# Down products of an MLP: seven products on quarters for eight pairs of feature chunks, and a gate by one SiLU

## Chip, cores and metric

One core of a Trainium2 chip. The time is the device time of one execution in microseconds, the median of several runs; the shares come from one profiled execution. TensorE (PE) multiplies, VectorE (DVE) and ScalarE (ACT) do elementwise work, GpSimd (POOL) a few small steps and the accumulating transfers, SyncE (SP) issues most of the other DMAs.

## The reference, cut to what matters

x is 2048 rows by 512 columns, all in float32; F is 1376.

```python
xn = layernorm(x)
s = linear_attention(xn, wqkv, wo)         # 32 heads of 16, features max(t,0)+exp(min(t,0))
hs = shift(gelu(layernorm(xn) @ w1)) @ w2  # quarters of the columns shifted by +1, -1, +2, -2 rows
x1 = xn + hs
h2 = gelu(layernorm(x1) @ w3) @ w4         # the MLP: 512 -> 1376 -> 512
out = x + s * silu(x1 + h2)
```

## The kernel before, in words

The kernel writes down some 5000 operations in a program order and lets a planner of its own (`Plan`, lines 88 to 395) choose the issue order. Every operation has an engine, a busy time and a latency by formula. TensorE's operations get a nominal time by adding their busy times up; the others get a due time from the operation that needs them. `emit` then goes forward, and takes again and again the operation that can start first, by due time among those. A DMA has a modelled landing. A TensorE operation that opens a new PSUM bank may go ahead of its place by 6 us at most, and only while two banks are free. `SOONER` moves single due times by hand. What comes out is a fixed instruction stream for each engine, with semaphores between.

Buffers come from pools: "p" has 96 of 128 x 516 words, for nearly everything; "h" six of 256 columns; PSUM has four banks "acc" and four "mm". A load into a "p" buffer is issued at most about 14 us ahead of need, and later when few buffers are free.

Precision: every float32 matrix is split into a rounded high part and the rest, and a product is three matmuls, high by high, high by low, low by high (`products`, line 478). All matmuls stand on line 148, so the profile tells them apart by tiles: the left name of a row is the PSUM tile.

Rows are worked in four blocks of 512 rows, a block being four tiles of 128. Up to about 228 us the kernel does the attention's sums over all rows (k, q, the Gram matrix g) and the token mixing (h, and the w2 product); x1 is kept in DRAM (`x1d`), its layer norm, turned, too. Then the loop at line 1441 does the MLP of the four blocks, one after the other. F is eleven chunks of 128 features, the last of 96; five pairs (s, s + 5) and the last alone. For each block:

- `up_last` (line 1133): the last chunk's up product, PSUM tile `a`, 24 matmuls of 256 columns.
- `up_pair` (line 1149): the up product of one pair of chunks by Strassen's scheme in Winograd's form (`seven`, line 883): seven products of 256 x 256 blocks for eight, each two contraction chunks by three split matmuls, 42 matmuls of 256 columns, in three banks (`pa`, `pb`, `pe`). Results go through GELU on ScalarE twice, once to the high part and once in full, and the low part is their difference.
- `down` (line 1168): the down product of a chunk, 512 columns wide, for the four row tiles, summed over all eleven chunks in four banks `acc`. The chunks of a group are issued one group after their up product; the last two groups (three in block 3) at the end.
- `turn_q`, `forms_q`, `attend_pair`: the attention's output for two row tiles each, again by `seven` (tiles `pas`, `pbs`, `pes`, result `so`), among groups two to five.
- `gate` (line 1246): x1 is fetched (`xo`) and added to the bank, then th = tanh(t/2), so = so * t, th = (th + 1) * so. The factor 1/2 of the SiLU stands in the mask of the attention (line 1403). x is added by an accumulating DMA on POOL's queue or, for the last two tiles, by VectorE, and the tile is stored.

In block 3 the fourth tile is summed in two halves of 256 columns, the second in a bank `accx` of its own, with x1 added there by an identity matmul: the last gate works on a half tile straight from PSUM.

w3's forms stay in buffers through all blocks; w4's split parts are made in block 0, kept in DRAM (`w4d`) and fetched again for each block (`load_w4`, line 1107), four transfers of 256 KB per pair.

Of the kernel before, what the change touches and what calls it, by code (L numbers as in the profile page):

```python
# [82 lines left out]
class Op:  # L83
    __slots__ = ("eng", "busy", "lat", "emit", "pre", "post", "tiles", "opens", "two", "table", "patience", "soon", "loads",
                 "nom", "due", "ready", "at", "end", "mb", "order")


class Plan:
# [9 lines left out]
    def add(self, eng, busy, lat, reads, writes, emit, two=False, table=None, mb=0.0):  # L98
# [4 lines left out]
        op.patience, op.soon = self.patience, False  # L103
# [55 lines left out]
    def act(self, out, src, func, scale=1.0, bias=None, total=None):  # L159
        nc = self.nc  # L160
        psum = out.tile.psum or src.tile.psum
        lat = (.15 if psum else .195) + out.n / 1200
        lat += .092 * (isinstance(scale, View) + isinstance(bias, View)) + (.095 if total is not None else 0)
        table = 0 if func == AF.Exp else 1 if func in (AF.Gelu_apprx_tanh, AF.Tanh) else None

        def emit():
            kw = {} if bias is None else {"bias": get(bias)}
            if total is not None:
                kw["accum_out"] = total.get()
            nc.scalar.activation(out.get(), src.get(), func, scale=get(scale), **kw)  # L170

        self.add("ACT", lat - .1, lat, [src, scale, bias], [out] + ([] if total is None else [total]), emit, table=table)
# [32 lines left out]
    def load(self, out, src, eng="SP"):  # L205
        mb = out.n * P * 4 / 1e6
        e = self.nc.scalar if eng == "ACT" else self.nc.sync
        self.add(eng, .42, 0, [], [out], lambda: e.dma_start(out.get(), src), mb=mb)

    def store(self, dst, src):  # L210
        mb = src.n * P * 4 / 1e6
        if isinstance(dst, View):
            return self.add("SP", .42, 0, [src], [dst], lambda: self.nc.sync.dma_start(dst.get(), src.get()), mb=mb)
        else:
            self.add("SP", .42, 0, [src], [], lambda: self.nc.sync.dma_start(dst, src.get()), mb=mb)

    def fetch(self, out, src):

        mb = out.n * P * 4 / 1e6
        self.add("SP", .42, 0, [src], [out], lambda: self.nc.sync.dma_start(out.get(), src.get()), mb=mb)  # L220

    def gather(self, out, src, share=1.0):

        mb = out.n * P * 4 / 1e6 * share
        return self.add("POOL", .8, 0, [src, out], [out],
                 lambda: self.nc.gpsimd.dma_start(out.get(), get(src), accum_op=ALU.add), mb=mb)  # L226

# [42 lines left out]
    def emit(self, first, lead, reserve, window, ahead, table=()):  # L270
# [20 lines left out]
        while left:  # L291
# [70 lines left out]
            if op.mb:  # L362
                soft = e == "POOL"
                late = min(.92, 1.03 * max(0.0, dma - s))
                dma = max(dma, s + (.97 if soft else .06)) + op.mb * (4.59 if soft else 3.43)
                op.end = max(dma + (1.89 if soft else 1.29) + late, s + (4.08 if soft else 2.08 if op.loads else 2.2))
                under[soft].pop(0)
                under[soft].append(op.end)
# [30 lines left out]
def linear_attn_gated_by_mixer(  # L399
# [29 lines left out]
    EARLY = (), ()  # L429
    SUMS = "DVE"  # L430
# [8 lines left out]
    counts = {"w": 2, "p": 96, "h": 6, "sm": 10, "ab": 2, "acc": 4, "mm": 4}  # L439
# [202 lines left out]
    def join_a(b):  # L642

        t = ABC[b] = pl.new("ab", f"abc{b}", F32, BT + W)
        a = EDGE + b * BT - 2
        pl.fetch(t.all, arow[:, a:a + BT + W].via(lambda ap: ap.to_broadcast([P, BT + W])))
# [32 lines left out]
    def make_u(b):  # L679

        m = piece(f"um{b}")
        pl.fetch(m, mrow[:, b * BT:(b + 1) * BT].via(lambda ap: ap.to_broadcast([P, BT])))
# [58 lines left out]
    class Turned:  # L741
# [15 lines left out]
        def take(self):  # L757
# [3 lines left out]
            for n in range(nb):  # L761
# [4 lines left out]
                pl.fetch(dst, src)  # L766
# [212 lines left out]
    x1d = {i: memory(f"x1d{i}") for i in range(NT)}  # L979
# [18 lines left out]
    def mixed(i, xv):  # L998
# [4 lines left out]
        pl.store(x1d[i].all, xv)  # L1003
# [26 lines left out]
    w3d = {s: memory(f"w3d{s}", NF * 512) for s in range(NS)}  # L1030
    w4d = {f: memory(f"w4d{f}", 1024) for f in range(FB)}
    AF3, W4, YT, H3 = {}, {}, {}, {}
# [74 lines left out]
    def load_w4(b, f):  # L1107
        n = rows(f)
        if b == 0 and f not in early_f:
# [3 lines left out]
        for k, v in enumerate(W4[b, f]):  # L1113
            pl.fetch(v.f32, w4d[f][:n, k * 512:(k + 1) * 512])

# [33 lines left out]
    def up_pair(b, s):  # L1149
        hi, lo = zip(*(rounds(f"f{b}_{f}") for f in (s, s + NS)))  # L1150
        full = [piece(f"gf{b}_{f}") for f in (s, s + NS)]
        c1, c2 = full
# [15 lines left out]
    def down(b, f, j, a, c=0, wd=512):  # L1168
        hi, lo, n = H3[b, f]
        left = both((hi.rows(n), lo.rows(n)), j * P, (j + 1) * P)  # L1170
        products(a[:, :wd], [left + both(W4[b, f], c, c + wd)], f == FIRST, f == FINAL)

# [65 lines left out]
    def attend_pair(i):  # L1238
        o1, o2 = SO[i], SO[i + 1] = piece(f"so{i}"), piece(f"so{i + 1}")
        ps = seven(f"s{i}", [o1.cols(0, TH), o1.cols(TH, 512), o2.cols(TH, 512)],  # L1240
                   lambda x, y: [QF[i][x][c] + M[y][c] for c in range(2)])
        pl.act(o2.cols(0, TH), ps, AF.Copy)

    XO, XR, GT, XL = {}, {}, {}, {}

    def gate(i, a, o=0, w=512, late=False, by_dma=True, whole=False):
        cs = o, o + w
        if o == 0:
            XO[i], GT[i] = XL.get(i) or piece(f"xo{i}"), piece(f"th{i}")
            if late and i not in XL:  # L1250
                pl.fetch(XO[i], x1d[i].all)
            if not by_dma:
                XR[i] = piece(f"xr{i}")
                pl.load(XR[i], x[i * P:(i + 1) * P, :])
        t, so, th = XO[i].cols(*cs), SO[i].cols(*cs), GT[i].cols(*cs)
        if whole:
            t = a[:, :w]
        elif late:
            pl.tt(t, a[:, :w], t, ALU.add)
        else:  # L1260
            pl.act(t, a[:, :w], AF.Copy)
            pl.gather(t, x1d[i].all, 1.4)
# [3 lines left out]
        if by_dma:  # L1266
            pl.gather(th, x[i * P:(i + 1) * P, :])
        else:
            pl.tt(th, th, XR[i].cols(*cs), ALU.add)
        pl.store(out[i * P:(i + 1) * P, o:o + w], th)  # L1270
# [99 lines left out]
    fill = [lambda f=f: make_w4(f) for f in early_f] + [lambda s=s: make_pair(s) for s in early_s]  # L1370
# [32 lines left out]
    pool(.4, [], bmask.all, lambda: g.memset(bmask.all.get(), 0.5))  # L1403
# [31 lines left out]
    while fill:  # L1435
        fill.pop(0)()
    turn_y(0)
    load_last()
    load_w4(0, FB - 1)
    load_pair(0)  # L1440
    for b in range(NQ):
        A = [pl.new("acc", f"acc{b}_{j}", F32, 512) for j in range(QT)]
        last = b == NQ - 1
        B = [(A[-1], 0), (pl.new("mm", "accx", F32, 512), D // 2)] if last else []
        groups = [(FB - 1,)] + [(s, s + NS) for s in range(NS)]
        keep = 3 if last else 2
        for n, fs in enumerate(groups):
            if b == 0 and 0 < n < NS:
                load_pair(n)
            if n < NS:  # L1450
                for f in groups[n + 1]:
                    load_w4(b, f)
            elif not last:
                load_w4(b + 1, FB - 1)
            if n == 0:
                up_last(b)
            else:
                up_pair(b, n - 1)
            if b == 0 and n == 1:
                forms_m()  # L1460
            pairs = []
            if n > 0:
                for k in range(2):
                    if n == (2, 3)[k]:
# [3 lines left out]
                    if n == (4, 5)[k]:  # L1468
                        pairs.append(b * QT + 2 * k)
            if n > 0 and n - 1 < len(groups) - keep:  # L1470
                for f in groups[n - 1]:
                    for j in range(QT - len(B) // 2):
                        down(b, f, j, A[j])
                    for a, o in B:
                        down(b, f, QT - 1, a, o, D // 2)
                    while pairs:
                        attend_pair(pairs.pop())
            while pairs:
                attend_pair(pairs.pop())
        rest = [f for fs in groups[len(groups) - keep:] for f in fs]  # L1480
        if not last:
            turn_y(b + 1)
            for f in rest:
                for j in range(QT):
                    down(b, f, j, A[j])
            for j in range(QT):
                gate(b * QT + j, A[j], late=True)
        else:
            i, (a, o) = b * QT + QT - 1, B[-1]
            XL[i] = piece(f"xo{i}")  # L1490
            pl.fetch(XL[i], x1d[i].all)
            t = piece(f"xi{i}", F32R)
            hi, lo = t.cols(0, TH), t.cols(TH, 512)
            rounded(hi, lo, XL[i].cols(o, o + TH))
            pl.patience = 0.0
            for j in range(QT - 1):
                for f in rest:
                    down(b, f, j, A[j])
                gate(b * QT + j, A[j], late=True, by_dma=j < 2)
            for a, o in B:  # L1500
                if o:
                    for v in (hi, lo):
                        pl.mm(a[:, :TH], identr.all, v, False, False)
                for f in rest:
                    down(b, f, QT - 1, a, o, D // 2)
                gate(b * QT + QT - 1, a, o, D // 2, late=True, by_dma=False, whole=o > 0)

    SOONER = (
# [3 lines left out]
    )  # L1512
    pl.emit(first=6.0, lead={"p": 14.0, "w": 14.0, "ab": 10.0}, reserve={"p": 20, "w": 1, "ab": 0}, window=12.0,
# [38 lines left out]
```

## Time and profile before

| | us |
|---|---|
| Time before, median of 3 runs | 514.07 (512.39 to 514.64) |
| The profiled execution, its time | 512.43 |
| Its span (first to last instruction) | 510.7 |
| TensorE busy | 502.9 |
| VectorE busy | 426.3 |
| ScalarE busy | 348.9 |

Busy time of TensorE counts from the start of a matmul to its modelled end; since matmuls overlap, a run of them is measured by its whole length over its count. The windows view gives each engine's busy time in a stretch, and behind it, in brackets, the number of its instructions. Rows of a timeline read: start, duration, engine and line, operation, output <- inputs, shape.

### The profile page before, as it was taken

The numbers are of one execution on the slowest core, as the hardware profiler recorded it, in microseconds if no ns is written. First come the engines' busy times: TensorE is split into PE (matmuls) and PEld (weight loads), VectorE is DVE, ScalarE is ACT, GpSimd is POOL, SyncE is SP. The second block draws the span as 40 slices with busy tenths as digits, with TensorE's granted clock in tenths as the row PEclk, the third lists the DMA queues.
The fourth block names the chain that finished last, engine by engine and source line by source line (L and its number), as shares of the span: only waits on it lengthen the run. The fifth ranks groups of instructions, "written<-read, shape, count | busy, mean of one in ns | idle before, by whom it ended". The sixth has DMA issues, their size and how long they took to land.

```text
span 510.7 us, 8948 instructions
## 1 busy us (share of the span) xinstructions
PE 502.9 (98%) x2972; PEld 437.9 (86%) x2972; DVE 426.3 (83%) x885; ACT 348.9 (68%) x703; POOL 91.2 (18%) x145
## 2 busy tenths in 40 slices
PE   9998999999999999999999999999999999999995
PEld 7777777898888788889989898999898998999985
DVE  6999999999699986999999978956779656898645
ACT  5899699676697785866876668655488453765621
POOL 1258411663134122021000020000020000200000
PEclk9999999999999999999999999999999999999999
DMA  8889947189994799799767758475495595758604
GB/s 270 310 185 226 303 151 167 41 201 295 278 284 92 239 292 270 199 271 313 247 204 205 224 137 280 160 215 154 164 230 183 181 222 166 182 185 265 195 14 111
DMA packets 76619, 106.17 MB, mean 208 GB/s; under 512 B 8224, under 2 KB 31292, under 8 KB 76572
## 3 DMA queue, kind: packets, MB, share of 16 engines
q1 hardware_dynamic: 68940, 91.70, 56.4%
q0 software_dynamic: 7632, 13.90, 16.1%
q8 instruction: 23, 0.38, 0.3%
q14 instruction: 24, 0.20, 0.1%
HBM read 67.41 MB, written 29.77 MB: 190 GB/s over the span
## 4 chain that ended last, share of the span: by engine, by line
PE 86%; DVE 5%; ACT 5%; DMA 2%; issue 1%; SPq 1%; DVEq 0%; ACTq 0%
PE acc L148 23%; PE pb L148 11%; PE h L148 8%; PE g L148 7%; PE pbk L148 6%; PE pe L148 5%; PE pbm L148 4%; PE pbs L148 4%; PE pek L148 3%; PE pa L148 3%; PE pem L148 2%; PE a L148 2%; PE pes L148 2%; DMA y_1t<-y_1d 2%; PE pak L148 1%
## 5 line engine op out<-in xcount | busy, mean ns | idle before, releaser
L226 POOL DMA_DIRECT2D th<-in_x x14 | 12.2, 939 | 248.0 <-DVE so L192 64.8
L170 ACT ACTIVATE th<-xo 128x512 f32<-128x512 f32 (+1 forms) x16 | 9.8, 620 | 26.8 <-DVE xo L192 26.6
L192 DVE TENSOR_TENSOR xo<-acc,xo 128x512 f32<-128x512 f32 (+1 forms) x16 | 10.5, 671 | 16.9 <-PE acc L148 16.8
L170 ACT ACT_TABLE_LOAD x18 | 23.1, 1283 | 1.1 <-PEq L1543 0.8
L170 ACT ACTIVATE gf<-gf 128x512 f32<-128x512 f32 (+1 forms) x40 | 20.6, 525 | 0.8
L226 POOL DMA_DIRECT2D o<-x x16 | 14.0, 873 | 40.1 <-DVE o L192 15.5
L226 POOL DMA_DIRECT2D zacc<-kr x16 | 13.9, 867 | 40.6 <-DMA zacc<-kr 22.2
L170 ACT ACTIVATE p<-pb 128x256 f32<-128x256 f32 x20 | 7.6, 382 | 14.2 <-PE pb L148 14.0
L604 POOL TENSOR_TENSOR rs<-w,nhalf 128x4 f32<-128x4 f32 (+2 forms) x10 | 10.1, 1012 | 35.5 <-DVE w L197 32.6
L170 ACT ACTIVATE p<-pe 128x256 f32<-128x256 f32 x20 | 7.7, 385 | 11.9 <-PE pe L148 11.9
L170 ACT ACTIVATE ht<-ht 128x512 f32<-128x512 f32 x16 | 9.7, 623 | 8.9 <-DVE ht L192 8.9
L192 DVE TENSOR_TENSOR gf<-pa,p 128x256 f32<-128x256 f32 x20 | 8.4, 420 | 7.8 <-PE pa L148 7.5
L170 ACT ACTIVATE x<-x,nm,rs 128x512 f32<-128x512 f32 x16 | 12.9, 807 | 2.5 <-DVE nm L202 2.5
L598 DVE BATCH_NORM_STATS2 st<-o 128x6 f32<-128x512 f32 x16 | 10.9, 686 | 3.5 <-DMA o<-x 3.4
L192 DVE TENSOR_TENSOR gf<-u,pe 128x256 f32<-128x256 f32 x20 | 8.2, 410 | 6.5 <-PE pe L148 6.5
L202 DVE SCALAR_TENSOR_TENSOR kr<-kt,kr 128x512 f32<-128x512 f32 x16 | 10.9, 688 | 1.8 <-ACT kt L170 1.7
L170 ACT ACTIVATE y<-o,nm,rs 128x512 f32<-128x512 f32 x16 | 11.9, 807 | 0.5 <-DVE nm L202 0.5
L192 DVE TENSOR_TENSOR ht<-h,abc 128x512 f32<-128x512 f32 x16 | 10.9, 683 | 0.8 <-PE h L148 0.6
L202 DVE SCALAR_TENSOR_TENSOR pq<-pq,qr 128x512 f32<-128x512 f32 x12 | 8.1, 683 | 4.1 <-ACT pq L170 4.0
L170 ACT ACTIVATE u<-pb 128x256 f32<-128x256 f32 x20 | 7.7, 383 | 5.5 <-PE pb L148 5.5
L202 DVE SCALAR_TENSOR_TENSOR th<-th,so 128x512 f32<-128x512 f32 (+1 forms) x17 | 10.9, 653 | 0.5
L202 DVE SCALAR_TENSOR_TENSOR pq<-pq,rd 128x512 f32<-128x512 f32 x16 | 10.9, 688 | 0.2
(1679 smaller groups left out, 2235.5 us busy)
## 6 DMA issues: line engine op xcount, KB each, us to landing
w_s<-in_w SPq DMA_DIRECT2D x28, 256.0 KB, 4.3
x<-in_x SPq DMA_DIRECT2D x16, 256.0 KB, 5.3
zacc<-kr POOLq DMA_DIRECT2D x16, 256.0 KB, 5.9
o<-x POOLq DMA_DIRECT2D x16, 256.0 KB, 4.9
x1d<-o SPq DMA_DIRECT2D x16, 256.0 KB, 4.2
xo<-x1d SPq DMA_DIRECT2D x16, 256.0 KB, 5.0
xt<-in_xt SPq DMA_DIRECT2D x15, 256.0 KB, 5.0
out<-th SPq DMA_DIRECT2D x15, 256.0 KB, 3.4
```

Of the source, the lines that this page charges most:

```text
L148: lambda: nc.tensor.matmul(out.get(), lhs.get(), rhs.get(), start=start, stop=stop, skip_group_check=more))
L170: nc.scalar.activation(out.get(), src.get(), func, scale=get(scale), **kw)
L192: self.vec(eng, out, [a, b], lambda: self.e(eng).tensor_tensor(out.get(), a.get(), b.get(), op=op), True)
L202: lambda: self.nc.vector.scalar_tensor_tensor(out.get(), a.get(), get(s), b.get(), op0=op0, op1=op1),
L226: lambda: self.nc.gpsimd.dma_start(out.get(), get(src), accum_op=ALU.add), mb=mb)
L598: pl.add("DVE", .62, .69, [xv], [st], lambda: nc.vector.bn_stats(st.get(), xv.get()))
L604: lambda: g.tensor_tensor(out.get(), src.get(), nh.get(), op=ALU.pow))
```

## The change

In blocks 1 to 3 the down product of a pair is done by the same seven-product scheme, over row halves, the two chunks, and column halves: two pairs in block 1, three in block 2, three in block 3 (`SEVENS`), ahead of the last chunk and the ordinary pairs. Each product is two row tiles by three split matmuls of 256 columns. Four of the seven are summed over the pairs, straight in four accumulators that each hold a quarter of the block (256 rows x 256 columns in the two halves of one bank); a11 b11 is summed in a fifth bank from "mm". At the last pair of a block a chain follows in that bank: its content is copied out for quarter 11, s2 t2 of all pairs is added, it is copied for 12, s3 t3 is added, and it is copied for 21 and 22. x1 is added to these copies by accumulating DMAs. The remaining chunks of blocks 1 to 3 are added to the quarter accumulators with 256-column matmuls (`plain`).

The left forms are sums of GELUs, so a pair now makes a11, a12, a22 and s1 to s4, each split; the right forms t1 to t4 of w4 are made once (`make_t4`), t1 and t4 used at once, all four kept in DRAM (`w4t`).

The gate takes one SiLU on ScalarE and one multiply on VectorE; the mask holds 1.0. In blocks 1 to 3 it works on quarters.

The planner gets other DMA rates by kind of transfer, SiLU as a third table, 98 buffers in "p" (two that held `abc` apart join it), and another `SOONER` list.

```diff
-    counts = {"w": 2, "p": 96, "h": 6, "sm": 10, "ab": 2, "acc": 4, "mm": 4}
+    counts = {"w": 2, "p": 98, "h": 6, "sm": 10, "acc": 4, "mm": 4}
+    SEVENS = 0, 2, 3, 3
+    FIRST7 = 1
-        table = 0 if func == AF.Exp else 1 if func in (AF.Gelu_apprx_tanh, AF.Tanh) else None
+        table = {AF.Exp: 0, AF.Gelu_apprx_tanh: 1, AF.Silu: 2}.get(func)
+    RATE = {"load": 2.92, "fetch": 3.5, "row": 4.18, "turn": 5.7, "store": 2.44, "gather": 5.79}
+    def make_t4(b, s):
+        r1, r2 = piece(f"w4_{s}_s0"), piece(f"w4_{s}_s1")
+        for r, f in ((r1, s), (r2, s + NS)):
+            pl.load(r, w4[f * P:(f + 1) * P, :])
...
+        right([r.cols(k * TH, (k + 1) * TH) for r in (r1, r2) for k in range(2)], lambda k: place[k])
+        for n, (src, a, z) in enumerate(((fa, "t1", "t4"), (fb, "t2", "t3"))):
+            hl = rounds(f"w4_{s}_{n}")
+            rounded(*hl, src)
...
+    def load_group(b, s):
...
+        for name in ("b11", "t4", "b21", "t1", "b22"):
+            load_form(b, s, name)
+    def up_pair(b, s):
+        if s >= SEVENS[b]:
+            up_plain(b, s)
+            return
...
+        ps = seven(f"{b}_{s}", z, lambda x, y: [AF3[s][x][c] + YT[b][y][c] for c in range(2)])
...
+        def keep(name, v, src):
+            t = piece(f"f{b}_{s}{name}", F32R)
+            f[name] = t.cols(0, TH), t.cols(TH, 512)
+            pl.act(f[name][0], src, AF.Gelu_apprx_tanh)
+            pl.act(v, src, AF.Gelu_apprx_tanh)
+            split(f[name][1], v, f[name][0])
+        pl.act(z[1], z[1], AF.Gelu_apprx_tanh)
+        keep("a11", z[0], z[0])
+        pl.tt(n3, z[0], z[1], ALU.subtract)
+        keep("a22", z[2], z[2])
+        pl.tt(n1, z[1], z[2], ALU.add)
+        pl.tt(n2, n1, z[0], ALU.subtract)
+        hl = rounds(f"f{b}_{s}t")
+        rounded(*hl, s23)
...
+        keep("a12", z[3], ps)
+        pl.tt(n4, z[3], n2, ALU.subtract)
+        hl = rounds(f"f{b}_{s}s")
+        rounded(*hl, s14)
...
+    STREAM = ("a1", "a11", "b11"), ("a4", "a22", "t4"), ("a2", "a12", "b21"), ("a5", "s1", "t1"), ("a3", "s4", "b22")
+    CHAIN = None, ("s2", "t2"), ("s3", "t3")
+    def into(regs, left, right, first):
+        for j in range(2):
+            out, own = regs[j]
+            start = first and (own or j == 0)
+            products(out, [both(left, j * P, (j + 1) * P) + right], start, more=not start,
+                     behind=out.tile.all if first else None)
+    def stream(b, acc, s, which=STREAM):
+        for a, x, y in which:
+            into(acc[a], F4[b, s][x], G4[b, s, y], s == 0)
+    def plain(b, acc, f, which):
+        hi, lo, n = H3[b, f]
+        for a in which:
+            t, d = QUARTER[a]
+            left = both((hi.rows(n), lo.rows(n)), t * TH, (t + 1) * TH)
+            into(acc[a], left, both(W4[b, f], d * TH, (d + 1) * TH), False)
+    def downs(b, acc, s, which=("a4", "a2", "a5", "a3")):
...
+            if s < SEVENS[b] - 1:
+                stream(b, acc, s)
+            else:
+                for n in range(3):
+                    stream(b, acc, s, (STREAM[:1], STREAM[1:3], STREAM[3:])[n])
+                    chain(b, n)
+                c = piece(f"c5_{b}")
+                pl.act(c, acc["a5"][0][0].tile.all, AF.Copy)
+                pl.tt(EV[b]["12"], c, EV[b]["12"], ALU.add)
...
+    def chain(b, n):
...
+        for s in range(SEVENS[b]) if n else ():
+            x, y = CHAIN[n]
+            load_form(b, s, y)
+            into(UC[b], F4[b, s][x], G4[b, s, y], False)
+        for k in (("11",), ("12",), ("21", "22"))[n]:
...
+            pl.act(e[k], t.all, AF.Copy)
+            pl.gather(in2(e[k]), x1)
-        pl.act(th, t, AF.Tanh, scale=0.5)
-        pl.tt(so, so, t, ALU.mult)
-        pl.stt(th, th, 1.0, so, ALU.add, ALU.mult)
+        pl.act(th, t, AF.Silu)
+        pl.tt(th, th, so, ALU.mult)
-    pool(.4, [], bmask.all, lambda: g.memset(bmask.all.get(), 0.5))
+    pool(.4, [], bmask.all, lambda: g.memset(bmask.all.get(), 1.0))
-        groups = [(FB - 1,)] + [(s, s + NS) for s in range(NS)]
+        n7 = SEVENS[b]
+        groups = list(range(n7)) + ["last"] + list(range(n7, NS))
```

In block 3 each quarter is finished by itself and gated while the next is summed (`a2`, `a5`, `a3`, then the two row halves of `a4`, the second in a bank of its own with x1 from an identity matmul).

More of the change, by code (lines that the diff above doesn't have):

```diff
@@ L977, in mixer @@
         forms(b)
-    x1d = {i: memory(f"x1d{i}") for i in range(NT)}
+    x1d = [memory(f"x1d{b}", 512, QT * P) for b in range(NQ)]
     YD = {}
@@ L1002, in mixed @@
         moments(f"st2{i}", xv, mv2[:, 2 * i:2 * i + 2])
-        pl.store(x1d[i].all, xv)
+        pl.store(x1d[b].cut([(j * 512, (j + 1) * 512)], 512, lambda ap: ap[j * P:(j + 1) * P, :]), xv)
         if j < QT - 1:
@@ L1238, in attend_pair @@
     def attend_pair(i):
[L1239 to L1255, printed above, removed]
+        b, k = divmod(i, QT)
@@ L1274, in linear_attn_gated_by_mixer @@
+        pl.act(th, t, AF.Silu)
+        pl.tt(th, th, so, ALU.mult)
+        j0, j1 = o // TH, (o + w) // TH
+        if xr is None:
+            pl.gather(in2(th), quarter(x, b, h, d, j0, j1))
+        else:
+            pl.tt(th, th, xr.cols(o, o + w), ALU.add)
+        pl.store(quarter(out, b, h, d, j0, j1), in2(th))
     warm = bank("warm")
@@ L1478, in linear_attn_gated_by_mixer, with whole @@
[L1478 to L1481, printed above, removed]
+                downs(b, acc, groups[n - 1])
+            for k in range(2):
+                if n == SAT[b][k]:
+                    attend_pair(b * QT + 2 * k)
+        rest = groups[len(groups) - keep:]
+        def whole(k):
+            return acc[k][0][0].tile.all
+        if b < FIRST7:
             turn_y(b + 1)
-            for f in rest:
-                for j in range(QT):
-                    down(b, f, j, A[j])
+            for s in rest:
+                downs(b, acc, s)
@@ L1486, in linear_attn_gated_by_mixer @@
             for j in range(QT):
-                gate(b * QT + j, A[j], late=True)
-        else:
[L1489 to L1492, printed above, removed]
+                gate_tile(b, j, acc[j].all)
+        elif not last:
+            turn_y(b + 1)
+            for s in rest:
+                downs(b, acc, s)
+            gate(b, 0, 0, whole("a2"))
+            gate(b, 1, 1, whole("a5"))
+            gate(b, 0, 1, whole("a3"))
+            gate(b, 1, 0, whole("a4"))
+        else:
+            e = EV[b]
+            xr = {}
+            for h, d in ((0, 1), (1, 0)):
+                xr[h, d] = piece(f"xr{h}{d}")
+                pl.load(in2(xr[h, d]), quarter(x, b, h, d))
+            t = piece("xi", F32R)
@@ L1493, in linear_attn_gated_by_mixer @@
             hi, lo = t.cols(0, TH), t.cols(TH, 512)
-            rounded(hi, lo, XL[i].cols(o, o + TH))
+            rounded(hi, lo, e["21"].cols(TH, 512))
             pl.patience = 0.0
[L1496 to L1501, printed above, removed]
-                    for v in (hi, lo):
[L1503 to L1506, printed above, removed]
+            for a, h, d in (("a2", 0, 0), ("a5", 1, 1), ("a3", 0, 1)):
+                for s in rest:
+                    downs(b, acc, s, (a,))
+                gate(b, h, d, whole(a), xr=xr.get((h, d)))
@@ new lines, in linear_attn_gated_by_mixer @@
+            for j in range(2):
+                r = acc["a4"][j][0]
+                if j:
+                    for v in (hi, lo):
+                        pl.mm(r, identr.all, v, False, False, more=True)
+                for s in rest:
+                    for f in (FB - 1,) if s == "last" else (s, s + NS):
+                        ah, al, n = H3[b, f]
+                        left = both((ah.rows(n), al.rows(n)), TH + j * P, TH + (j + 1) * P)
+                        products(r, [left + both(W4[b, f], 0, TH)], False, more=True)
+                gate(b, 1, 0, r, j * TH, TH, xr=xr[1, 0], whole=j > 0)
```

211 lines of the change are left out of this document (147 added, 64 removed), and 7 rows, old and new, of the table SOONER.

## The prediction

> **What bounds the kernel now.** First the page: the span, the busy time of each engine, and the chain that ended last.
>
> ```profile
> span 510.7 us, 8948 instructions
> PE 502.9 (98%) x2972; PEld 437.9 (86%) x2972; DVE 426.3 (83%) x885; ACT 348.9 (68%) x703; POOL 91.2 (18%) x145
> ...
> PEclk9999999999999999999999999999999999999999
> ...
> PE 86%; DVE 5%; ACT 5%; DMA 2%; issue 1%; SPq 1%; DVEq 0%; ACTq 0%
> ```
>
> TensorE is busy for 502.9 of 510.7 us at the full granted clock, and the chain lies on it. The waits of TensorE and the windows of the four MLP blocks (228 to 297, 297 to 366, 366 to 436, 436 to 505.6 us) say where the other 7.8 us are. The window's columns are PE, PEld, DVE, ACT and POOL busy, then clock, DMA share and GB/s.
>
> ```profile
> PE h L148 <- ACT w_0h L170: 1.3, 1, 1.3
> PE warm L148 <- POOL ones L511: 1.0, 1, 1.0
> PE pbs L148 <- ACT u2s L170: 0.3, 1, 0.3
> ```
>
> ```profile
> 228.00:297.00 69.00, 69.00 (x452) 62.25 (x450) 65.69 (x135) 47.57 (x107) 2.23 (x2) 1.00 0.76 237
> 297.00:366.00 69.00, 69.00 (x452) 62.40 (x451) 50.52 (x101) 43.30 (x90) 3.50 (x4) 1.00 0.65 189
> 366.00:436.00 70.00, 69.69 (x453) 62.42 (x452) 51.31 (x102) 43.14 (x90) 3.50 (x4) 1.00 0.70 187
> 436.00:505.60 69.60, 69.60 (x486) 64.31 (x484) 50.11 (x101) 37.52 (x83) 5.22 (x6) 1.00 0.58 165
> 505.60:510.70 5.10, 0.00 (x1) 0.00 (x0) 1.30 (x4) 0.38 (x1) 0.00 (x0) 0.96 0.35 126
> ```
>
> 5.1 us lie behind the last product, 1.0 at the start, 1.3 at one wait and 0.3 in block 2: that is 7.7. So inside the blocks that the change touches TensorE never stops, and time there is the number of products times their spacing. Block 0 matters as a yardstick: VectorE was busy for 65.69 of 69 us there and the DMA engines for 0.76 of the time, and TensorE lost nothing.
>
> The spacing comes from the chain in order of time (start, us, engine and tile, count), where pieces of one shape stand alone. "a" is 256 columns wide, "acc" 512.
>
> ```profile
> 287.67 9.72 PE acc L148 x42
> 297.39 2.83 PE a L148 x24
> ...
> 356.82 9.53 PE acc L148 x41
> 366.35 2.81 PE a L148 x24
> ...
> 426.13 9.99 PE acc L148 x43
> 436.12 2.83 PE a L148 x24
> ...
> 503.25 2.37 PE accx L148 x20
> ```
>
> 512 columns: (9.72 + 9.53 + 9.99) / 126 = 0.2321 us. 256 columns: (2.83 + 2.81 + 2.83) / 72 = 0.1176 us, 0.0016 over half. From "a" of block 1 to that of block 2 are 366.35 - 297.39 = 68.96 us. Its products make 318 x 0.1176 (24 of the last chunk, 210 of five pairs, 84 of two attention pairs) + 132 x 0.2321 = 68.03; so about 0.9 us a block hide as small slips between products that still count as busy.
>
> **The change, part by part: TensorE.** A pair of feature chunks is now two chunks by four row tiles by three split products: 24 products of 512 columns, 24 x 0.2321 = 5.570 us. Afterwards it is seven products by two row tiles by three: 42 of 256 columns, 42 x 0.1176 = 4.939. Saved: 0.631 for each of the five pairs in blocks 1 and 2. In block 3 the fourth tile is already cut in halves, so a pair costs 18 x 0.2321 + 12 x 0.1176 = 5.589 and 0.650 is saved, three times. Together 5 x 0.631 + 3 x 0.650 = 5.11 us.
>
> What remains ordinary is cut to quarters too (plain): a chunk goes from 12 x 0.2321 = 2.785 to 24 x 0.1176 = 2.822. Blocks 1 and 2 have 7 + 5 such chunks, 12 x 0.037 = 0.44; block 3 has five, each 2.822 - 2.794 = 0.028, 0.14. Net on TensorE: 5.11 - 0.58 = **4.5 us less**. Block 0, the up products and the attention pairs keep theirs.
>
> Here a page would turn the sign. The trace first: 0.1176 against 0.2321 us, so two halves cost 1.01 of a whole. The Trainium skill, "TensorE: Matmul & The Clock Gate", section "Back-to-back issue gap", gives a sustained stream of weight load and matmul about 81 ns at 128 columns and 131 at 512, so that 256 would by a line between them (an estimate from that page) be near 98, and 42 x 98 = 4.1 us would replace 24 x 131 = 3.1. The trace disagrees.
>
> **The tail.** The last half tile goes from PSUM to the output by these (engine by engine):
>
> ```profile
> 505.32 0.28 PE L148 MATMUL accx<-w_9h,f_9l 128*128 128x256 f32 x1
> 505.64 0.38 ACT L170 ACTIVATE th<-accx 128x256 f32<-128x256 f32 x1 [1.48 <-PE accx L148]
> 506.05 0.42 DVE L192 TENSOR_TENSOR so<-so,accx 128x256 f32<-128x256 f32 x1 [0.42 <-ACT th L170]
> 506.51 0.42 DVE L202 SCALAR_TENSOR_TENSOR th<-th,so 128x256 f32<-128x256 f32 x1
> 506.97 0.42 DVE L192 TENSOR_TENSOR th<-th,xr 128x256 f32<-128x256 f32 x1
> ```
>
> With SiLU one VectorE step goes: multiply, add x, store. The store is issued one step, 506.97 - 506.51 = **0.46 us**, earlier. Against it, the last stretch between gates shrinks from 20 products (2.37 us) to 17 (2.00), and three VectorE steps and one of ScalarE of the half tile before still fit into it.
>
> **VectorE and ScalarE.** The shapes are in the page:
>
> ```profile
> L170 ACT ACTIVATE th<-xo 128x512 f32<-128x512 f32 (+1 forms) x16 | 9.8, 620 | 26.8 <-DVE xo L192 26.6
> ...
> L170 ACT ACT_TABLE_LOAD x18 | 23.1, 1283 | 1.1 <-PEq L1543 0.8
> ...
> L170 ACT ACTIVATE p<-pb 128x256 f32<-128x256 f32 x20 | 7.6, 382 | 14.2 <-PE pb L148 14.0
> ...
> L192 DVE TENSOR_TENSOR gf<-pa,p 128x256 f32<-128x256 f32 x20 | 8.4, 420 | 7.8 <-PE pa L148 7.5
> ...
> L202 DVE SCALAR_TENSOR_TENSOR kr<-kt,kr 128x512 f32<-128x512 f32 x16 | 10.9, 688 | 1.8 <-ACT kt L170 1.7
> ```
>
> A pair in sevens adds three splits and four sums of 256 columns on VectorE (the two wide splits stay two): 7 x 0.42 = 2.9 us. make_t4, once for each of three pairs, adds 4 x 0.42 + 2 x 0.69 = 3.1; the sum for quarter 12 adds 0.7 a block; a gate loses 0.69, four to a block. Block 2, the fullest: 51.3 + 3 x 2.9 + 3.1 + 0.7 - 2.8 = 61.0 of about 68 us. That is 90%, below block 0's 95%, which cost TensorE nothing. ScalarE adds per pair 3.9 - 2.8 = 1.1 us (seven GELUs of 256 at 0.38 and two copies of 0.62, for two GELUs of 512 and four of 256), and a block five reads of a bank at 0.62 and two table loads: 43.1 + 3.3 + 3.1 + 2.6 + 1.3 (make_t4) = 53 of 68. All of it lies beside TensorE; uncovered, block 2's extra 9.7 us of VectorE alone would swallow the gain.
>
> **Table loads.** Tanh and GELU share one; SiLU gets a table of its own: two loads at each of three block ends, one at the last, seven. The turn from block 0 to block 1 and one switch to Exp and back on ScalarE:
>
> ```profile
> 296.13 1.27 ACT L170 ACTIVATE th<-xo 128x512 f32<-128x512 f32 x2 [3.83 <-DVE xo L192]
> 298.02 1.23 ACT L170 ACTIVATE th<-xo 128x512 f32<-128x512 f32 x2 [0.63 <-DVE xo L192]
> ...
> 307.19 1.28 ACT L170 ACT_TABLE_LOAD   x1
> 308.48 0.72 ACT L170 ACTIVATE pq<-qv,rs 128x512 f32<-128x512 f32 x1
> ```
>
> ScalarE sat idle 3.83 us ahead of the first gate, so that load (1.28) is covered. The load back stands ahead of the next block's first GELU. Below it costs nothing; above, all four back and forth that aren't covered, 4 x 1.28 = 5.1. I take 0, nearest to the idle row, since a pair's GELU feeds products that are issued one group later. Tanh stood between GELUs without a load (none from 296 to 307 us). The Trainium skill, "ScalarE: Activation LUTs", section "What ACT_TABLE_LOAD costs", puts a switch at about 2.66 us, drain included, and by it the seven would be 18.6 us of ScalarE. The trace disagrees: the next instruction starts 1.29 us after the load does.
>
> **Waits that are added.** (1) The chain of the seven-product form uses one bank three times: TensorE writes a11 b11, ScalarE copies it, TensorE adds s2 t2, ScalarE copies, TensorE adds s3 t3. Each copy (0.62) must end before TensorE goes on in that bank; two streams, 12 x 0.1176 = 1.41 us, are placed between. Queued behind a waiting product is all of TensorE. Below 0; above, a copy that stands behind a table load and a GELU, 1.28 + 0.62 + 0.62 - 1.41 = 1.1 us, six times, 6.7. Nearest is the one wait of TensorE on such a copy, 0.3 (pbs on u2s); I take half, 0.15 x 6 = **0.9**. (2) That bank comes out of the pool of four which up and attention products use. Three are what one seven takes, so the next may wait for an eviction: below 0, above one copy (0.38) for each of the 21 sevens of blocks 1 to 3 (15 up, 6 attention), 8 us; I take 0, as down products lie between. (3) Transfers: per pair seven right forms of 256 KB for four, less six kept in place, plus six loads and twelve stores of make_t4: 24 - 6 + 18 = 36 transfers, 9.4 MB over three blocks. At 187 GB/s with 0.70 busy, 9.4 MB take some 35 us of all engines in 208 us, 0.17 more: about 0.81 against block 0's 0.76. I take 0; what it costs when a landing shows is the second rival. (4) Four x1d loads a block become accumulating transfers of POOL, which is busy for 3.5 of 70 us there, with landings (last column) as long as SP's:
>
> ```profile
> xo<-x1d SPq DMA_DIRECT2D x16, 256.0 KB, 5.0
> ...
> th<-in_x POOLq DMA_DIRECT2D x14, 256.0 KB, 5.1
> ```
>
> They are issued a group or more ahead of the gates: 0, and one landing, 5.1, if a gate at the end of block 3 waited for it.
>
> (5) All of the order is planned anew with other DMA rates: it may give back the 1.3 us wait and some of the 0.9 a block, or lose as much: plus or minus 3, taken as 0.
>
> Sum: 512.43 (the profiled execution: span 510.7 and 1.7 around it) - 4.5 - 0.46 + 0.9 = 508.4, **4.1 us less**. That execution lies 1.6 under the median of the runs, 514.07; against the median it is **510.0**.
>
> **The rivals.** A measurement of this kernel tells 0.5%, 2.6 us, from no change.
> - The gain is eaten by small waits: of (1), (2) and the slips, 2 to 6 us come true. Against: TensorE's waits in four blocks sum to 0.3. For: VectorE at 90% and ScalarE at 78%. 511.5 to 516, within 0.5% for the most part.
> - **Buffers, slower.** The w3 forms (35), the last chunk (2), y forms (16), attention forms (14) and zb hold 68 of 98 buffers through a block. A pair in sevens holds 7 left forms for 4 and 5 right ones for 4, and s2, s3 until the chain. With three pairs that is 2 + 7 + 7 + 5 + 5 = 26 of 30 before any scratch. Then right forms can only be fetched when a buffer comes free, and a landing shows:
>
> ```profile
> w_6l<-w4d SPq DMA_DIRECT2D x3, 256.0 KB, 6.4
> w_2h<-w4d SPq DMA_DIRECT2D x3, 256.0 KB, 2.8
> ```
>
>  The point is 0.6 us per pair (the gain), 0.95 for slower by 0.5%. One landing of about 4.5 in each of three blocks gives 13.5: 523; only the short ones, 8.4: 518. Against: the first pairs run before attention work and before the next y forms are made.
> - SiLU's loads on the path: 5.1 us, 515.
> - More than the arithmetic: the new order also returns 2 to 4 us of waits and slips. 506 to 508.
> - Halves cost more than 0.1176 in these streams, as when the weight load set the spacing: at 5.570 / 42 = 0.133 the pair breaks even. Three rows of 24 and one of 20 (0.1185) say no.
>
> **How the numbers follow.** Forecast (508 to 511.5) 0.56; more than that 0.10; eaten 0.20; buffers 0.10; loads 0.03; halves 0.01, a time near 514. Faster: 0.56 + 0.10 = 0.66. Same: 0.20 + 0.03 + 0.01 = 0.24. Slower: 0.10. The range takes in the forecast, the larger gain and the eaten case up to 514.5; it leaves out buffers, loads and the end of the eaten case: 505.5 to 514.5.
>
> **What would show it.** Right: about 315 more matmul records (18 for each of five pairs, 12 for three, 12 for twelve chunks, 9 for five); block 1 near 68.96 - 1.26 + 0.26 = 68.0 us; TensorE's waits under 2 us; seven more table loads. Wrong: TensorE waiting on a w4t or w4d landing (buffers), on ScalarE's copies out of the shared bank (chain), or on a GELU behind a table load; or the saving there, and lost again ahead of 228 us, where only the new order can be the cause.

## The result, and the profile after

Over 20 runs each the kernel takes 510.78 us after and 512.41 before; the medians lie 1.6 us apart. The estimated ratio is 0.9963 (95% interval 0.9949 to 0.9976), so 1.9 us less, between 1.2 and 2.6. The forecast was 4.1 less. The page after, in the lines shown of before:

```profile
span 509.2 us, 9828 instructions
PE 500.7 (98%) x3287; PEld 453.0 (89%) x3287; DVE 443.6 (87%) x945; ACT 374.3 (74%) x756; POOL 106.6 (21%) x157
...
PE 93%; DMA 3%; ACT 2%; DVE 1%; SPq 0%; issue 0%; ACTq 0%
...
L170 ACT ACT_TABLE_LOAD x26 | 33.4, 1283 | 5.8 <-DMA w4t<-w_1l 2.3
```

There are 3287 - 2972 = 315 more matmuls, as counted, and eight more table loads (seven were forecast). TensorE's waits after, then the windows of the four blocks and of the tail:

```profile
PE h L148 <- ACT w_0h L170: 1.2, 1, 1.2
PE warm L148 <- POOL ones L518: 1.0, 1, 1.0
PE k L148 <- ACT u_1h L170: 1.0, 1, 1.0
PE w1m L148 <- DVE w1ml L192: 0.5, 1, 0.5
```

```profile
229.25:298.25 69.00, 69.00 (x452) 62.52 (x451) 68.42 (x144) 49.37 (x109) 2.24 (x2) 1.00 0.82 261
298.25:366.50 68.25, 68.25 (x571) 67.84 (x570) 54.73 (x115) 47.56 (x102) 8.34 (x8) 1.00 0.93 246
366.50:435.40 68.90, 68.85 (x567) 67.93 (x566) 58.14 (x125) 52.84 (x111) 9.60 (x8) 1.00 0.88 233
435.40:504.20 68.80, 68.74 (x570) 68.13 (x569) 53.98 (x116) 47.06 (x100) 11.96 (x10) 1.00 0.73 188
504.20:509.20 5.00, 0.35 (x3) 0.14 (x2) 1.24 (x3) 0.38 (x1) 0.00 (x0) 1.00 0.48 159
```

All four waits lie ahead of the MLP. They sum to 3.7 us, over the 2 that the forecast named as a sign, but inside the MLP the view shows none. Inside the blocks TensorE is "busy" without a gap, as before, and yet the blocks shrank by less than the products say: that view lists only gaps in TensorE's busy time. A busy TensorE does not show what it loses. This timeline of block 2 does (start, duration, tile <- inputs):

```profile
395.29 0.28 PE L148 MATMUL uc<-w_t,f_1th 128*128 128x256 f32 x1
395.52 0.39 PE L148 MATMUL a<-w_0l,f_2a 128*128 128x256 f32 x1
395.74 0.28 PE L148 MATMUL a<-w_0h,f_2a 128*128 128x256 f32 x1
395.86 0.28 PE L148 MATMUL a<-w_0l,f_2a 128*128 128x256 f32 x1
```

Read the starts: 0.23, 0.22, 0.12 apart. A product came 0.11 late, the next another 0.10, and both intervals lie under the modelled durations of 0.28 and 0.39. So all lengths below are taken from the starts: a block runs from its first up product to the next block's; its work is its products times 0.1176 or 0.2321; the rest is its slip. (Starts are counted from the first instruction, 0.31 us into the span.)

| us | MLP starts | block 1 | block 2 | block 3 | slip of blocks 1, 2, 3 |
|---|---|---|---|---|---|
| before | 227.88 | 68.96 | 69.77 | 69.48 | 0.93, 1.74, 1.11 |
| after | 229.25 | 68.25 | 68.92 | 68.66 | 1.21, 2.59, 2.10 |

From last product to the end, 510.7 - 505.32 = 5.38 became 509.2 - 504.27 = 4.93; the fused step is gone:

```profile
504.27 0.28 PE L148 MATMUL a4x<-w_9h,f_9l 128*128 128x256 f32 x1
...
505.01 0.42 DVE L192 TENSOR_TENSOR th<-th,so 128x256 f32<-128x256 f32 x1 [0.42 <-ACT th L170]
505.46 0.42 DVE L192 TENSOR_TENSOR th<-th,xr 128x256 f32<-128x256 f32 x1
```

In these two executions, then: work 4.5 less, tail 0.45 less, slips of blocks 1 to 3 2.1 more, and the MLP begins 1.4 later; together 1.5, the difference of the spans. Two questions: is the later start real, and what makes the slips?

### The profile page after: what moved, and what is told of

It is laid out like the page before. It is cut to its first block, busy times and chain, and to the rows that moved or that the text cites. A ratio compares the mean times of both kernels' runs of the same rounds, so it can differ in the third digit from the quotient of the medians.

```text
span 509.2 us, 9828 instructions
## 1 busy us (share of the span) xinstructions
PE 500.7 (98%) x3287; PEld 453.0 (89%) x3287; DVE 443.6 (87%) x945; ACT 374.3 (74%) x756; POOL 106.6 (21%) x157
## 4 chain that ended last, share of the span: by engine, by line
PE 93%; DMA 3%; ACT 2%; DVE 1%; SPq 0%; issue 0%; ACTq 0%
PE a L148 15%; PE pb L148 11%; PE h L148 9%; PE g L148 7%; PE pbk L148 7%; PE acc L148 6%; PE pe L148 6%; PE pbm L148 5%; PE pbs L148 5%; PE uc L148 3%; PE pek L148 3%; PE pa L148 3%; PE pem L148 2%; PE pes L148 2%; PE k L148 2%; PE pak L148 2%
## 5 line engine op out<-in xcount | busy, mean ns | idle before, releaser
L224 POOL DMA_DIRECT2D th<-in_x x14 | 15.5, 1468 | 173.6 <-DMA w4t<-w_0h 60.6
L224 POOL DMA_DIRECT2D e<-x1d x12 | 14.4, 1302 | 56.8 <-ACT e L170 27.1
L170 ACT ACTIVATE gf<-gf 128x256 f32<-128x256 f32 (+1 forms) x48 | 22.0, 466 | 0.5
L611 POOL TENSOR_TENSOR rs<-w,nhalf 128x4 f32<-128x4 f32 (+2 forms) x10 | 11.5, 1149 | 29.3 <-DVE w L197 28.4
L170 ACT ACTIVATE th<-e 128x512 f32<-128x512 f32 (+1 forms) x12 | 7.2, 612 | 8.7 <-DVE e L192 8.7
L192 DVE TENSOR_TENSOR e<-a,e 128x512 f32<-128x512 f32 (+1 forms) x12 | 7.6, 663 | 6.7 <-PE a L148 6.7
L192 DVE TENSOR_TENSOR th<-th,so 128x512 f32<-128x512 f32 (+1 forms) x17 | 10.7, 652 | 2.5 <-ACT th L170 2.5
```

The lines of the kernel that those rows point to most:

```text
L192: self.vec(eng, out, [a, b], lambda: self.e(eng).tensor_tensor(out.get(), a.get(), b.get(), op=op), True)
L611: lambda: g.tensor_tensor(out.get(), src.get(), nh.get(), op=ALU.pow))
```

## The experiments

The theory at the start: the new order ahead of the MLP costs 1.4 us, and the slips come from evictions of up and attention products that are late because ScalarE and VectorE have more to do. Rivals: the start is chance; the slips come from SiLU's table loads, from the chain's bank, from a store that ScalarE waits for, or from the half-width products themselves. Most kernels keep the planned order exactly and change only what one operation issues; block lengths of such kernels agree to some hundredths of a microsecond where the edit does nothing (an exception, a stray wait in block 2 of before, is met below), so the blocks of one profiled execution tell more than a median time. All ratios are to before, timed again beside each group of kernels. The edits are shown shortened.

**Order ahead of the MLP, in the changed kernel and in the one before.**

```diff
+        if op.order < 2117:     # after: the landing formula and due times of before; before: those of after
```

> The changed kernel, planned with the DMA landings and the hand-set due times of the kernel before for all operations ahead of the MLP (the first 2117), the rest as changed. Theory (the new order ahead of the MLP costs 1.4 us; the products save 4.5, of which about 1.2 go to more slips between products in blocks 2 and 3): the MLP begins near 227.9 instead of 229.25 us and the time falls by about 1.4 us, to 509.4. Rival (the later start of the MLP is chance of one profiled execution): same time as the changed kernel, 510.8.

> The kernel before, planned with the new DMA landings and the new due times for the operations ahead of the MLP alone. Theory (the new order ahead of the MLP costs 1.4 us): the MLP begins near 229.2 instead of 227.9 us, time 513.8. Rival (chance): 512.4, as before.

Measured: 515.02, ratio to before 1.0043 (1.0021 to 1.0065), and 514.65, ratio 1.0039 (1.0023 to 1.0055). The MLP began at 231.7 and 230.4. Both transplants are slower than the kernel they came from, and neither tests what it was made for. The planner gave each an order of its own: of the 1137 products ahead of the MLP, 120 stand at another place in the first than in before, and 135 in the second than in after. In the first, so do 715 of the 2150 products of the MLP, against after; its profiled execution, 519.44 us, is the longest of its twelve and holds 4.8 us more slip in blocks 1 to 3 than after. What settles the question is other executions with exactly the two orders. In five of the order of before (before, and below the halves, the load, the planned load and the gate) the MLP begins at 227.88, 228.28, 228.31, 228.44 and 230.08, mean 228.6; in seven of the order of after (after, and the six kernels below made from it) between 228.33 and 229.25, mean 228.8. **The 1.4 us were chance**, to within the 2 us by which executions of one order differ.

**SiLU's tables.** Same order, GELU issued in the gates:

```diff
+        func = AF.Gelu_apprx_tanh if func == AF.Silu else func
```

> The changed kernel in the same planned order, with GELU issued in place of SiLU in the gates: the SiLU is left out, and with it its table. Rival (SiLU's table loads make the slips of blocks 2 and 3): these blocks get 1.0 to 1.5 us shorter in sum, time 509.5. Theory (the slips come from ScalarE's and VectorE's other added work and late evictions): 0.3 us or less, 510.6.

Measured 510.55, ratio 0.9954 (0.9936 to 0.9973). Blocks 68.05, 68.90, 68.66: block 1 gains 0.20, blocks 2 and 3 nothing. The rival falls.

**The chain's bank.** Same order:

```diff
-            pl.act(e[k], t.all, AF.Copy)
+            pl.act(e[k], t.all, AF.Copy, instead=zacc.all)   # also the copy of a5
```

> The changed kernel in the same order, but the copies out of the shared bank (quarters 11, 12, 21, 22) and out of a5 read a constant in SBUF instead: the sums of that bank are left out of the output, and TensorE never waits for those copies nor they for TensorE. Rival (the chain's bank makes the slips): blocks 1 to 3 get 0.5 to 1.3 us shorter in sum, time 509.6. Theory (late evictions of the up and attention products): 0.3 us or less, 510.6.

Measured 512.30, ratio 0.9988 (0.9972 to 1.0004). Blocks 68.33, 70.60, 68.63. Blocks 1 and 3 do not get shorter, so the waits at that bank, step (1) of the forecast, cost these blocks no length that shows. Block 2 is 1.7 us longer; a likely reason is a wait elsewhere. ScalarE in block 2, this kernel first, then after:

```profile
384.53 0.38 ACT L170 ACTIVATE u<-pb 128x256 f32<-128x256 f32 x1
388.02 1.28 ACT L170 ACT_TABLE_LOAD   x1 [3.11 <-DMA w4t<-w_1l]
389.31 0.42 ACT L170 ACTIVATE f_2a<-gf 128x256 fp32r<-128x256 f32 x1
```

```profile
384.87 0.39 ACT L170 ACTIVATE u<-pb 128x256 f32<-128x256 f32 x1
387.56 1.28 ACT L170 ACT_TABLE_LOAD   x1 [2.31 <-DMA w4t<-w_1l]
388.86 0.42 ACT L170 ACTIVATE f_2a<-gf 128x256 fp32r<-128x256 f32 x1
```

ScalarE stands still until a store of make_t4 has landed, because the left form f_2a is to go into the buffer that the store reads. The block began 0.36 us earlier in the first kernel and the landing came 0.46 later. Its TensorE then waited on ScalarE, which it does not after:

```profile
PE a L148 <- ACT gf L170: 0.8, 1, 0.8
PE pb L148 <- ACT u L170: 0.5, 1, 0.5
```

**The store.** So is the wait of 2.3 us in after part of block 2's slip? Same order, no buffer waits for a store:

```diff
                 op = pl.store(to, in2(v.f32))
+                op.emit = lambda to=to: nc.sync.dma_start(to.get(), in2(zacc.all).get())
```

> The changed kernel in the same order, but make_t4's stores read a constant: the t forms that are fetched later are left out, and no buffer of w4's split parts waits for a store to land. In the changed kernel ScalarE idles 2.3 us in block 2 until such a store has landed. Theory 3 (this wait makes block 2's slips): block 2 falls from 68.9 to about 68.1 us, time 510.0. Rival: block 2 the same within 0.2, time 510.7.

Measured 510.70, ratio 0.9969 (0.9955 to 0.9983); block 2 68.87. ScalarE:

```profile
384.32 0.38 ACT L170 ACTIVATE u<-pb 128x256 f32<-128x256 f32 x1
384.72 1.28 ACT L170 ACT_TABLE_LOAD   x1
386.58 0.42 ACT L170 ACTIVATE f_2a<-gf 128x256 fp32r<-128x256 f32 x1 [0.58 <-DVE gf L192]
```

The GELU comes 1.7 us sooner in its block, and the block is as long as ever. A wait of 2.3 us there costs nothing; the run before suggests that one of 3.1 costs more than a microsecond.

**Half-width products.** The kernel before, same order, each down product of blocks 1 to 3 cut in two:

```diff
+                for k in range(2):
+                    nc.tensor.matmul(out.cols(k * 256, k * 256 + 256).get(), lhs.get(), ...
```

> The kernel before in the same order, with each 512-column down product of blocks 1 to 3 (363 of them) issued as two of 256 columns. By the spacings alone 363 x 0.0031 = 1.1 us more: blocks 1 to 3 from 208.2 to 209.3 us, time 513.7. Theory 1 (a stream of 256-column products has no reserve in its weight loads, so that each late arrival shows, as in the changed kernel): about 1 us more than that, 210.3 and 514.7. Theory 2 (the slips come from the added work of ScalarE and VectorE): 209.3.

Measured 513.58, ratio 1.0019 (1.0002 to 1.0037). Blocks 69.43, 69.57, 69.73, in sum 208.7, with slips of 0.99, 1.13 and 1.05. There are 0.6 us less than before's, because before's own block 2 held one stray wait of 0.48. Counted without it, the halves cost 208.7 - 207.7 = 1.0, the 1.1 of their spacing, and no slips. Theory 1 falls, and the prices of the forecast's products stand.

**The added elementwise work alone.** The kernel before, same order:

```diff
+                for n in range(3): nc.scalar.activation(hi[1].cols(0, TH).get(), c2.cols(0, TH).get(), AF.Copy)
                 was()
+                for n in range(7): nc.vector.tensor_tensor(o.get(), a.get(), h.f32.get(), op=ALU.subtract)
```

> The kernel before in the same order, with the added elementwise work alone: for two pairs in block 1 and three each in blocks 2 and 3, seven more VectorE splits and three more ScalarE copies of 256 columns, which rewrite values already there. Theory 2 (this work makes the slips): blocks 1 to 3 get about 1 us longer in sum, 209.2, time 513.4. Theory 1 (no reserve in the weight loads of 256-column streams): 0.2 us or less, time 512.6.

Measured 533.91, ratio 1.0418 (1.0399 to 1.0438): 21 us, 2.6 for each of eight pairs. Its block 2 in the windows, TensorE's waits, and one such place on VectorE and on TensorE:

```profile
369.80:446.40 76.60, 70.20 (x452) 62.29 (x451) 58.17 (x122) 46.05 (x99) 3.50 (x4) 1.00 0.59 171
```

```profile
PE pb L148 <- DVE gf L192: 12.7, 8, 3.1
```

```profile
409.43 2.44 DVE L1173 TENSOR_TENSOR f_7l<-gf,f_7h 128x256 fp32r<-128x256 f32 x7
411.79 0.41 DVE L192 TENSOR_TENSOR gf<-pa,p 128x256 f32<-128x256 f32 x1
...
413.06 0.41 DVE L192 TENSOR_TENSOR gf<-u,pe 128x256 f32<-128x256 f32 x1
...
414.44 0.42 DVE L192 TENSOR_TENSOR gf<-pb,p 128x256 f32<-128x256 f32 x1
```

```profile
411.74 0.39 PE L148 MATMUL acc<-w_2h,f_2h 128*128 128x512 f32 x1
414.91 0.39 PE L148 MATMUL pb<-yt42h,w_b 128*128 128x256 f32 x1 [2.78 <-DVE gf L192]
```

VectorE is busy for 58.17 us in this block and for 58.14 in the changed kernel's block 2, which is 7.7 us shorter. Same load, other places: here seven steps stand in one piece of 2.44 us, the three evictions queue behind it, and TensorE waits for the last.

**The same work, known to the planner.**

```diff
+            op.busy += 7 * .34
+            op.lat += 7 * .34      # ScalarE's copies likewise
```

> The kernel before with the same added elementwise work as in the run that cost 21 us, but with the work's duration told to the planner, which orders everything anew. Theory (the work can be hidden where the order knows of it): blocks 1 to 3 within 2 us of before in sum, time 513.5. Rival (there is no room for it): over 518.

Measured 524.58, ratio 1.0240 (1.0224 to 1.0256). Planning takes back 9 of 21 us and no more; the piece cannot be cut, and the waits move to the down products:

```profile
PE acc L148 <- DVE f_6l L1173: 2.0, 2, 1.4
PE pbs L148 <- ACT q12h L170: 1.5, 1, 1.5
PE acc L148 <- DVE f_7l L1173: 1.3, 1, 1.3
```

**The gate alone.** The kernel before, same order:

```diff
-    tanh(t / 2); so = so * t; th = (th + 1) * so
+    op.emit = lambda: nc.scalar.activation(th.get(), t.get(), AF.Silu)   # then th = th * so
```

> The kernel before in the same order, with the gate of the change alone: SiLU for tanh, one VectorE multiply for a multiply and a fused step, 1.0 in the mask. Tail 0.46 us shorter, blocks the same within 0.2 us: time 511.9. Rival (SiLU's table loads stand ahead of GELUs): blocks longer by up to 1 us each, time 513 or more.

Measured 513.30, ratio 1.0014 (1.0002 to 1.0027). From the last product to the end 512.6 - 507.69 = 4.91, 0.47 less. Blocks 69.25, 69.28, 69.79: 0.3 more in blocks 1 and 3. So in the order of before the gate alone gains nothing: what the tail gives, the blocks take.

**Taking the work away from the changed kernel.** Two kernels in the same order, and one planned anew:

```diff
-            split(f[name][1], v, f[name][0]); pl.tt(n1 .. n4)
+            g.memset(out.f32.get(), 0.25)          # seven steps; the second kernel also two of ScalarE
-        pl.tt(n3, z[0], z[1], ALU.subtract)
+        pl.tt(n3, z[0], z[1], ALU.subtract, eng="POOL")   # third kernel, and n1
```

> The changed kernel in the same order, with the seven added VectorE steps of each pair in sevens (three splits, four sums of 256 columns) left out; GpSimd, idle there, fills their places with a constant, so these values are left out. Theory 2 (late evictions behind that VectorE work make the slips): blocks 2 and 3 fall from 68.9 and 68.7 by about 0.5 us each, time 509.7. Rival (the slips are those of the planned order, whatever VectorE does): both within 0.2 us, time 510.7.

> As the run without the seven VectorE steps, and of ScalarE's added work one GELU and one copy of 512 columns per pair are left out too. Theory 2: blocks 2 and 3 fall by about 0.9 us each against the changed kernel, to the slips of the kernel before (1.1 to 1.7), time 509.0. Rival: within 0.2 us, time 510.7.

> The changed kernel with two of the four sums of each pair in sevens on GpSimd instead of VectorE, the order planned anew. Theory 2: VectorE has 0.8 us less per pair, slips of blocks 2 and 3 fall by 0.3 us each, time 510.2. Rival (GpSimd's step is twice as long and stands in the chain that makes the left forms; any new order costs): 511.5 or more.

Measured 516.66, 515.15 and 518.79; ratios 1.0061 (1.0037 to 1.0084), 1.0051 (1.0031 to 1.0070) and 1.0116 (1.0089 to 1.0142). All three expectations missed, and for a reason of their own. GpSimd in the first and TensorE's waits in it, then GpSimd in the third:

```profile
L1252 POOL MEMSET f_1a<- 128x256 f32 x9 | 7.9, 1122 | 2.3 <-PE a L148 2.3
L1252 POOL MEMSET f_0a<- 128x256 f32 x9 | 6.3, 1237 | 31.6 <-DMA qv<-pqd 31.6
```

```profile
PE a L148 <- POOL f_1a L1252: 1.0, 1, 1.0
PE uc L148 <- POOL f_1a L1252: 0.8, 1, 0.8
```

```profile
L192 POOL TENSOR_TENSOR sf_1b<-gf 128x256 f32<-128x256 f32 x3 | 3.7, 1223 | 10.7 <-DVE w_1l L192 6.8 <-DVE f_0sl L192 3.9
L192 POOL TENSOR_TENSOR sf_1a<-gf,gf 128x256 f32<-128x256 f32 x3 | 3.3, 1111 | 3.0 <-PE uc L148 2.6 <-ACT qr L170 0.5
```

A sum of 256 columns takes 0.74 to 1.84 us on GpSimd in the third, against 0.42 on VectorE. The means of the constants mix records of 0.3 us with records of 0.8 to 2.1 us that overlap (those in a row start 0.25 us apart). TensorE waited for GpSimd in the first, and in the third for VectorE and ScalarE, 2.1 us at the longest. These runs do not test the theory, since GpSimd in place of VectorE brings delays of its own. No kernel beat the changed one beyond its interval.

## Why the forecast held and where it failed

- **What bounds the kernel; the products (4.5 us less): right.** The count is exact, and the run with halves confirms the spacing. The 81 and 131 ns that the Trainium skill, "TensorE: Matmul & The Clock Gate", section "Back-to-back issue gap", gives for 128 and 512 columns would have turned the sign; that run, with 1.0 us for 363 cut products, disagrees.
- **The tail (0.46): right**, 0.45 after and 0.47 with the gate alone.
- **Table loads at 0: nearly.** 0.2 us in block 1, nothing in blocks 2 and 3; the gate alone costs 0.3 in two blocks. Eight loads, not seven.
- **(1) the chain's bank, 0.9: wrong place.** Without those waits blocks 1 and 3 keep their length; about 0.3 us of slips stand behind its copies in after.
- **(3) transfers at 0, and the rival of the buffers.** The DMA share rose to 0.93, 0.88 and 0.73, over the 0.81 worked out for the mean of the three (0.85). A buffer did make an engine wait, for a store and not a fetch, and at 2.3 us without effect on the time. One longer such wait came with 1.7 us more in its block.
- **VectorE and ScalarE beside TensorE at 0: the step that failed.** The busy times came out about as forecast in block 2 (58.1 us on VectorE for 61.0, 52.8 on ScalarE for 53), so it was the conclusion from them that failed. Its argument was the share: block 0 carried 95% on VectorE and lost nothing (by the starts it lost 1.0 us, much like block 1). The added work on its own costs 21 us at the same share as in the changed kernel. A share says nothing of cover; what counts is what stands ahead of an eviction. The changed kernel has the work in single steps and loses little, but not nothing, and most of that behind ScalarE, as worked out below.
- **The size.** Slips of blocks 1 to 3 grew by 2.1 us (2.6 without the stray wait of before), where 0.9 were taken: 4.5 + 0.45 - 2.6 = 2.3 less, inside the measured 1.2 to 2.6. The rival that the gain is eaten by small waits is what came true, by half; the range held it. The forecast gave 0.66 to a gain of about 2.6 us or more, and the 1.9 measured lie below that. That the time, 510.78, came within 0.8 us of the forecast 510.0 is luck: the 4.1 were taken off 514.07, the median of three runs, where 20 runs gave 512.41.
- **(5) the new order, 0 plus or minus 3: open.** Ahead of the MLP it changed nothing beyond chance. Inside the MLP it can't be told apart from the added work. The two transplants, orders that neither kernel has, moved the time by 2 and 4 us, so the bound was not a wide one.

Where the slips lie can be counted from the starts: of 5.9 us in blocks 1 to 3 (3.8 before) 3.0 stand at up products (2.0), 1.6 at attention products (1.5), 1.1 at down products (0.2), and 0.2 at the last chunk's. Slips over 0.02 us are 69 for 42, 4.8 us for 3.0. Excluded as their cause are half-width products, the store, and but for some tenths the chain's copies and the tables.

What released them can be read from the semaphores of the two traces. At each of the 69 and of the 42 slips, the weight load of the late product, or of the one before it, followed within 0.05 us on the end of a step of ScalarE or VectorE that it had to wait for; of the other products 8 to 9% stand so. At the largest slip of after, the eviction p<-pe stood behind the SiLU of a gate, though its product had ended 0.3 us before (PEld are weight loads):

```profile
437.83 0.62 ACT L170 ACTIVATE th<-e 128x512 f32<-128x512 f32 x1
438.36 0.37 ACT L170 ACTIVATE p<-pe 128x256 f32<-128x256 f32 x1
438.78 0.19 PEld L148 LDWEIGHTS pe<-yb223h,w_s1h 128*128 128x128 f32 x1 [0.26 <-ACT p L170]
438.78 0.39 PE L148 MATMUL pe<-yb223h,w_s1h 128*128 128x256 f32 x1
439.00 0.28 PE L148 MATMUL pe<-yb223l,w_s1h 128*128 128x256 f32 x1
```

VectorE ended 23 of these waits, 1.6 us of slips (before 18 and 1.5). ScalarE ended 46, 3.1 us (before 24 and 1.5, 0.6 of them the stray wait). Of ScalarE's, 32 with 2.7 us began without a pause behind another step of ScalarE (before 8 with 0.9); those that began after a pause did not grow, 14 with 0.5 us (before 16 with 0.6). So the slips over 0.02 us grew where ScalarE's steps stand in line, and hardly at VectorE; the load run, whose waits were mostly VectorE's, lost its time in another way. Ahead of those 32 stood GELUs in place (gf<-gf, 0.7 us of slips), gates (th<-e, 0.4), the change's new splits f_1a, f_1th and w_1h (0.4), and others, most of them steps that before has too (1.1). That the added steps make that line, and not the new order of the old ones, **is argued, not shown**: the runs that should have taken the work away failed.

## What to carry to other kernels

Work that leaves the engine that bounds arrives as counted, if the spacing is taken from rows of the same shape. What it costs on the other engines is not read from their share of busy time but from what stands ahead of an eviction: here one piece of 2.4 us cost 2.6 a pair, and about the same work in single steps some 0.3. A TensorE that is 98% busy can still lose microseconds in slips of 0.1; count them from the starts, ask the semaphores which engine ended each wait, and compare kernels in a fixed order.

## What the runs showed of the hardware

- A product that starts late because its weight load had to wait is followed by one that is late too, and by a nearly constant time: in 14 such places of blocks 1 to 3, before and after, the first was 0.03 to 0.48 us late and the second 0.10 to 0.11 (once 0.08). In other places only the second is late.
- GpSimd took 0.74 to 1.84 us for a sum of 256 columns (16 in the run that moved two sums), against 0.42 on VectorE.
- The start of the MLP varied from 227.9 to 230.1 us between executions of one order, while the length of block 0, which follows, varied by 0.06 us.
